# Splitting one rounding in the last, narrower supertile of two feed-forward networks, and moving one copy from ScalarE to VectorE

## The chip, the cores and the metric

The kernel runs on one core of one Trainium2 chip. The metric is the device time of one execution in microseconds (us), the median of several runs. In what follows TensorE is PE in the rows (its weight loads are PEld), VectorE is DVE, ScalarE is ACT, GpSimd is POOL and SyncE is SP.

## The reference

Attention without softmax, then two feed-forward networks over the 6016 tokens that come out of it:

```
scores = (1/3008) * z @ z.T ; attn = max(scores, 0)**2 ; x0 = u * (attn @ v)      # 2 batches x 3008 tokens, 256 wide
h = x0 @ w_in1 ; x1 = (h - tanh(h)) @ w_out1                                     # 256 -> 2048 -> 256
h = x1 @ w_in2 ; g = h if h >= 1, 0 if h <= -1, else (h + 1)**2 / 4 ; out = g @ w_out2
```

All is fp32. The kernel keeps that precision by splitting each operand of a product into a rounded part (hi) and the rest (lo), and by multiplying hi with hi, hi with lo and lo with hi.

## The kernel before, in words

The first 440 us are attention; the change leaves them alone. Then the networks (net 0 and net 1) run as a list of 95 units, numbered here 0 to 94. A unit is one network, one supertile `s` of 1024 tokens, and one eighth `f` of the 2048 hidden features. Net 0 is units 0 to 47, net 1 units 48 to 94. There are six supertiles in each; the last has 896 tokens. A supertile is handled as two halves of `w` tokens, so `w` is 512, and 448 in the last one. The units of width 448 are 40 to 47 and 88 to 94; they are called narrow here.

A unit's first product is done by a scheme with seven block products instead of eight (`mult`, three matmuls each), in an order written out by hand in `Unit.emit`: A11 and A12 into banks Y and X, S1 into V, S2 onto Y, later S3 onto Y, A22 onto Y and S4 onto V. Between them ScalarE copies the state of Y to SBUF three times (`snap`: m1 after A11, u2 after S2, u3 after S3), because Y is added to again, and VectorE adds bank and copy to get the hidden values: `A.h` (half A, rows j = 0 and 1) and `B.h` (half B). So S2 may not start before m1 is copied, S3 not before u2, A22 not before u3.

The activation, the rounding and the second product of a unit are staggered: half A's `first` (tanh on ScalarE in net 0, a clamp on VectorE in net 1), `value` (VectorE) and, in net 0, `round` (ScalarE, makes `gha`) are issued at the end of the unit itself; half A's `rest` (VectorE, makes `gla`) and all of half B (`first`, `value`, `round` to `ghb`, `rest` to `glb`) are issued inside the next unit, where `p` is the unit before. The second product of unit `p` is `one` (8 matmuls of gha), `two` (4 of gla, 6 of ghb) and `three` (2 of ghb, 4 of glb), and its matmuls stand between the blocks of the next unit: A11, A12, S1, S2, `one`, S3, `two`, A22, S4, `three`. That makes 45 matmuls a unit. The order on each engine is the order of the code: no scheduler changes it, and each engine works its own list from the top.

`fill()` is called twice a unit. It pops one step of preparing the next supertile's input (`x_steps`: subtractions and rests on VectorE, roundings on ScalarE), or, where there is none, some steps of converting the next weights (`work`), or one transposition of results (`turn`, net 1). In net 0 every narrow unit has such steps; in net 1 there is one, the last step of `x_steps`, in the second call of unit 88, and there are four transpositions, in units 89 and 90. In the kernel before, the first `fill()` stands between `p.B.round` and `p.B.rest`, ahead of S3.

`empty` copies a finished supertile's four banks of sums (00, 10, 01, 11: feature half d, token half n) out of PSUM, two on ScalarE and two on VectorE, in the second unit of the next supertile; those banks are reused by the matmuls of `one` in that unit. At the networks' border this is unit 49.

Of the kernel before, what the change touches and what calls it, by code (L numbers as in the profile page):

```python
# [8 lines left out]
F32R = mybir.dt.float32r  # L9
# [6 lines left out]
P = 128  # L16
# [6 lines left out]
QT = 512  # L23
# [8 lines left out]
def attention_then_two_ffn(  # L32
# [40 lines left out]
    sp_p = ctx.enter_context(tc.tile_pool(name="split", bufs=3))  # L73
# [31 lines left out]
    def flush():  # L105
        for fn in deferred:
            fn()
        deferred.clear()
# [236 lines left out]
    for c in list(range(QC)) * B:  # L345
        n = 1 if c == QC - 1 else 2
# [11 lines left out]
    between = []  # L358
# [364 lines left out]
    def fill():  # L723

        if fills:
            step = fills.pop(0)
            for fn in step:
                if fn is not None:
                    fn()
            if len(step) == 1:  # L730
                work(CONVERT[1] / 2)
        else:
            work(CONVERT[1])
        due()

    def copy(out_, in_):
        nc.scalar.activation(out=out_, in_=in_, func=AF.Copy)  # L737

    def add(out_, x, bank):
        nc.vector.tensor_tensor(out=out_, in0=x, in1=bank, op=ALU.add)  # L740

    class Half:
# [26 lines left out]
                out=t, in0=self.h[self.at(j)], in1=t, op=ALU.subtract if self.net == 0 else ALU.max,  # L769
            )  # L770

        def round(self, js=(None,)):
            self.hi = sp_p.tile([P, 2, 512], F32R, tag="hi", name=f"gh{self.nm}")
            for j in js:
                copy(self.hi[self.at(j)], self.t[self.at(j)])

# [15 lines left out]
    class Unit:  # L792
# [59 lines left out]
        def emit(self, p, att=None):  # L852

            w = self.w
            before = p and p.net == 1 and p.f == 0 and p.s and p.before
            self.before = p
            self.late = self.net == 1 or att is not None
            one, two, three = p.parts_list if p else ([], [], [])
            Y = self.bank()
            self.mult(Y, A11, "b11", True)  # L860
            m1 = self.snap("m1", Y)
            if p and p.late:
                p.A.round()
            if p and p.before and p.before.net == 0:
                p.before.empty(0)
            X = self.bank()
            self.mult(X, A12, "b21", True)
            if p:
                if p.net == 1:
                    p.B.first()  # L870
                p.A.rest()
                p.B.first() if p.net == 0 else p.B.square(1 if before else None)
            if att:
                for fn in att[2][:5]:
                    fn()
            self.A = Half(self.net, w, "a")
            if not (p and p.late):
                add(self.A.h[:, 0, :w], m1, X[:, :w])
            V = self.bank()
            self.mult(V, S1, "t1", True)  # L880
            if att:
                for fn in att[2][5:]:
                    fn()
                got = []
                inside.append(lambda: self.mult(Y, S2, "t2"))
                inside.append(lambda: got.append(self.snap("u2", Y)))
                att[0]()
                u2 = got[0]
            else:
                self.mult(Y, S2, "t2")  # L890
                u2 = self.snap("u2", Y)
            if before:
                before.empty(1, lambda: p.B.square(0))
            if p:
                for j in (1, 0) if before else (None,):
                    p.B.value(j)
                if p.late:
                    add(self.A.h[:, 0, :w], m1, X[:, :w])
            for fn in one[:4] if before else one:
                fn()  # L900
            if p:
                p.B.round((1, 0) if before else (None,))
                if self.i > 1:
                    fill()
                else:
                    scales.pop()()
                    due()
                    due()
                p.B.rest()
            self.mult(Y, S3, "t3")  # L910
            if before:
                for fn in one[4:6] + two[:2] + one[6:]:
                    fn()
                two = two[2:]
            u3 = self.snap("u3", Y)
            add(self.A.h[:, 1, :w], u3, V[:, :w])
            if self.net == 1 or att:
                self.A.first()
            for fn in two:
                fn()  # L920
            if att:
                self.A.value()
                att[1]()
            if self.i > 1:
                fill()
            if self.net == 1:
                self.A.square()
            self.mult(Y, A22, "t4")
            self.mult(V, S4, "b22")
            self.B = Half(self.net, w, "b")  # L930
            if self.net == 0 and not att:
                self.A.first()
            copy(self.B.h[:, 1, :w], Y[:, :w])
            if not att:
                self.A.value()
            if att:
                flush()
            add(self.B.h[:, 0, :w], u2, V[:, :w])
            for fn in three:
                fn()  # L940
            if not self.late:
                self.A.round()
            if p and p.net == 1:
                p.empty(0)
            self.parts_list = self.parts()

        def empty(self, n, between=None):

            if self.f < NPF - 1:
                return  # L950
            w = self.w
            if self.net == 0:
                for n in range(2):
                    for d in range(2):
                        bank = accs.pop((0, self.s, d, n))[:, :w]
                        y = raw_p.tile([P, 512], F32, tag="raw", name=f"y{d}{n}")
                        if d:
                            nc.vector.tensor_copy(out=y[:, :w], in_=bank)
                        else:
                            copy(y[:, :w], bank)  # L960
                        nc.sync.dma_start(out=kept[1, self.s][:, d, n * w : (n + 1) * w], in_=y[:, :w])
                return
            o = wide_p.tile([P, 2, 16, 32], F32, tag="wide", name="ot")
            for d in range(2):
                bank = accs.pop((1, self.s, d, n))
                y = raw_p.tile([P, 512], F32, tag="raw", name=f"y{d}{n}")
                copy(y, bank)
                if between and d == 0:
                    between()
                fills.append((lambda d=d, y=y: self.turn(o, d, n, y),))  # L970
# [153 lines left out]
    with tc.manual_schedule():  # L1124
# [64 lines left out]
        def work(amount):  # L1189

            if not (converts or posts):
                return
            state["credit"] = min(state["credit"] + amount, 2.0)
            if posts:
                cost, fn = posts.pop(0)
                fn()
                state["credit"] -= cost
            while converts and state["credit"] > 0 and len(posts) < 3:
                if state["step"] == 0:
                    next(converts[0])  # L1200
                elif state["step"] == 1 and len(converts) > 1:
                    next(converts[1])
                state["step"] += 1
                cost = next(converts[0], None)
                if cost is None:
                    converts.pop(0)
                    state["step"] = 1
                else:
                    state["credit"] -= cost
# [45 lines left out]
        def due():  # L1255

            now = [fn for k, fn in later if k <= 0]
            later[:] = [(k - 1, fn) for k, fn in later if k > 0]
            for fn in now:
                fn()  # L1260
# [73 lines left out]
        p = None  # L1334
        for i, (net, s, f) in enumerate(units):
            if f == 0:
                more = (net, s + 1) if (net, s + 1, 0) in units else (1, 0) if net == 0 else None
# [9 lines left out]
            p = u  # L1347
# [70 lines left out]
```

## Time and profile before

| | us |
|---|---|
| median of 3 runs (1419.55 to 1420.5) | 1420.18 |
| the profiled execution | 1417.62 |
| its span, first to last instruction | 1415.8 |
| TensorE busy in the span | 1408.6 |
| VectorE busy | 1243.9 |
| ScalarE busy | 996.3 |
| mean granted TensorE clock (share of full speed) | 0.999 |

TensorE's matmuls are pipelined, so its busy share says little on how close it is to its limit. What it loses is better read from the spacing of its weight loads: in an undisturbed narrow unit 45 loads follow each other every 0.203 us, 9.12 us in all, in a 512-wide unit every 0.227 us, 10.20 us.

### The profile page before, as it was taken

The page shows a single profiled execution, that of the slowest core. Times are in us where ns is not written, and L with a number is a line of the kernel's source. Part 1 is how long each engine was busy: PE and PEld are TensorE (multiplying, and loading weights), DVE is VectorE, ACT ScalarE, POOL GpSimd, SP SyncE. Part 2 cuts the span into 40 slices and gives each one's busy share as a digit, 9 for nine tenths or more (in the row PEclk, how much of TensorE's full clock was granted, in tenths as well). Part 3 has the DMA queues.
Part 4 walks back from the last instruction along what each step waited for, and adds up shares of the span by engine and source line. Part 5 has one row for each costly group of instructions (what it writes and reads, how often), then busy time and mean ns, then how long its engine had stood idle before and what let it go on. Part 6 is the DMA issues. An engine that isn't in the chain of part 4 may idle for free.

```text
span 1415.8 us, 21846 instructions
## 1 busy us (share of the span) xinstructions
PE 1408.6 (99%) x8206; PEld 1173.7 (83%) x8206; DVE 1243.9 (88%) x1557; ACT 996.3 (70%) x1258; POOL 116.0 (8%) x169
## 2 busy tenths in 40 slices
PE   9999999999999999999999999999999999999998
PEld 7888888888888888888888889988888888888897
DVE  8888899788898989899889889989898898988887
ACT  8888758888765767667676767666666666666664
POOL 0111110022110010110201110000000000000000
PEclk9999999999999999999999999999999999999999
DMA  8788897599989557484847667572564653546461
GB/s 231 249 279 256 234 237 190 177 283 270 257 220 318 198 195 254 167 309 134 314 147 271 230 224 276 173 289 89 176 225 178 208 189 109 184 157 222 148 208 27
DMA packets 229546, 301.02 MB, mean 213 GB/s; under 512 B 111152, under 2 KB 166192, under 8 KB 229440
## 3 DMA queue, kind: packets, MB, share of 16 engines
q1 hardware_dynamic: 213088, 258.01, 57.6%
q0 software_dynamic: 11520, 40.96, 8.1%
q8 instruction: 64, 1.05, 0.3%
q10 hardware_dynamic: 4832, 0.66, 0.3%
q14 instruction: 42, 0.34, 0.1%
HBM read 225.77 MB, written 73.79 MB: 212 GB/s over the span
## 4 chain that ended last, share of the span: by engine, by line
PE 60%; issue 36%; DVE 1%; ACT 1%; DMA 1%; POOL 0%; SPq 0%; POOLq 0%; DVEq 0%; ACTq 0%
PE acc L825 17%; PE acc L537 16%; PE m L806 15%; PE acc L526 7%; PE sc L449 4%; DMA packed<-plin 0%; ACT r L475 0%; PE acc L532 0%; DVE lo L434 0%; PE warm L1122 0%; ACT hi L483 0%; DVE am L416 0%; POOL win L282 0%; POOL packed L295 0%; DVE lo L499 0%
## 5 line engine op out<-in xcount | busy, mean ns | idle before, releaser
L806 PE MATMUL m<-xht,w 128*128 128x512 f32 (+1 forms) x760 | 231.2, 385 | 0.0
L825 PE MATMUL acc<-ghb,w 128*128 128x512 f32 (+1 forms) x760 | 200.8, 386 | 0.0
L537 PE MATMUL acc<-hi,v 64*128 64x512 f32 (+1 forms) x1588 | 195.5, 382 | 0.2
L825 PE MATMUL acc<-gha,w 128*128 128x512 f32 (+1 forms) x760 | 187.1, 386 | 0.0
L537 PEld LDWEIGHTS acc<-hi,v 64*128 64x128 f32 x1588 | 148.5, 184 | 29.2 <-DVE y L592 1.3
L825 PEld LDWEIGHTS acc<-gha,w 128*128 128x128 f32 x760 | 142.4, 188 | 27.5 <-ACT y L737 0.4
L825 PEld LDWEIGHTS acc<-ghb,w 128*128 128x128 f32 x760 | 141.2, 188 | 29.0 <-ACT ghb L737 0.7
L806 PEld LDWEIGHTS m<-xht,w 128*128 128x128 f32 x760 | 142.7, 188 | 26.4
L806 PE MATMUL m<-xlt,w 128*128 128x512 f32 (+1 forms) x380 | 147.2, 387 | 0.0
L779 DVE TENSOR_TENSOR gla<-ta,gha 128x1024 fp32r<-128x1024 f32 (+1 forms) x95 | 114.4, 1204 | 36.7 <-ACT gha L737 36.0
L737 ACT ACTIVATE ghb<-tb 128x1024 fp32r<-128x1024 f32 (+3 forms) x100 | 99.8, 1004 | 63.0 <-DVE tb L768 63.0
L768 DVE TENSOR_TENSOR ta<-ha,ta 128x1024 f32<-128x1024 f32 (+1 forms) x95 | 114.2, 1202 | 32.6 <-ACT ta L764 27.5
L779 DVE TENSOR_TENSOR glb<-tb,ghb 128x1024 fp32r<-128x1024 f32 (+1 forms) x95 | 114.0, 1200 | 18.1 <-ACT ghb L737 17.9
L737 ACT ACTIVATE u<-m 128x512 f32<-128x512 f32 (+1 forms) x190 | 110.3, 580 | 26.3 <-PE m L806 25.4
L737 ACT ACTIVATE gha<-ta 128x1024 fp32r<-128x1024 f32 (+1 forms) x95 | 98.9, 1041 | 35.0 <-DVE ta L768 34.8
L768 DVE TENSOR_TENSOR tb<-hb,tb 128x1024 f32<-128x1024 f32 (+3 forms) x100 | 114.7, 1147 | 6.5 <-ACT tb L753 2.2
L806 PE MATMUL m<-xhb,w 128*128 128x512 f32 (+1 forms) x380 | 115.6, 386 | 0.0
L764 ACT ACTIVATE ta<-ta 128x1024 f32<-128x1024 f32 (+1 forms) x47 | 49.2, 1046 | 85.4 <-DVE ta L755 85.4
L537 PE MATMUL acc<-lo,v 64*128 64x512 f32 (+1 forms) x772 | 104.9, 382 | 0.2 <-DVE lo L434 0.2
L475 ACT ACTIVATE r<-sc 128x1024 f32<-128x1024 f32 (+1 forms) x83 | 84.4, 1016 | 28.4 <-PE sc L449 28.0
L825 PE MATMUL acc<-gla,w 128*128 128x512 f32 (+1 forms) x380 | 101.3, 386 | 0.0
L825 PE MATMUL acc<-glb,w 128*128 128x512 f32 (+1 forms) x380 | 101.1, 385 | 0.0
(139 smaller groups left out, 2566.1 us busy)
## 6 DMA issues: line engine op xcount, KB each, us to landing
w<-packed SPq DMA_DIRECT2D x288, 512.0 KB, 5.9
mir<-ax SPq DMA_DIRECT2D x50, 512.0 KB, 4.6
m<-mir SPq DMA_DIRECT2D x200, 128.0 KB, 4.6
xr<-kept SPq DMA_DIRECT2D x20, 512.0 KB, 6.9
packed<-phin POOLq DMA_DIRECT2D x16, 512.0 KB, 5.7
packed<-plin POOLq DMA_DIRECT2D x16, 512.0 KB, 6.1
widein<-in_moe_w_in_dram POOLq DMA_DIRECT2D x15, 512.0 KB, 6.9
wideout<-in_moe_w_out_dram POOLq DMA_DIRECT2D x15, 512.0 KB, 7.7
```

Source lines behind the costliest of these rows:

```text
L449: nc.tensor.matmul(ps[:, j, :n], zs[b, g][half, x, k0 : k0 + P], q[half, y, :n], start=(k == 0), stop=(k == 2))
L475: nc.scalar.activation(out=r[s], in_=ps[s], func=AF.Relu)
L526: nc.tensor.matmul(acc[d][h].rearrange("p (i q) -> p i q", i=2), lhsT, g[half, j], start=start, stop=stop)
L537: nc.tensor.matmul(acc[d][h][:, :n], lhsT, g[half, j, :n], start=start, stop=stop and (h == 1 or not closes))
L737: nc.scalar.activation(out=out_, in_=in_, func=AF.Copy)
L764: nc.scalar.activation(out=t, in_=t, func=AF.Square, scale=0.5, bias=0.5)
L768: nc.vector.tensor_tensor(out=t, in0=self.h[self.at(j)], in1=t, op=ALU.subtract if self.net == 0 else ALU.max,)
L779: nc.vector.tensor_tensor(out=self.lo[self.s], in0=self.t[self.s], in1=self.hi.bitcast(F32)[self.s], op=ALU.subtract)
L806: nc.tensor.matmul(bank[:, : self.w], self.win[wp][:, block, :], xop[self.net, self.s][x][xp], start=start and i == 0, stop=True, skip_gro ...
L825: nc.tensor.matmul(self.acc(d, n)[:, : self.w], self.wout[:, part, j, d * P : (d + 1) * P], g[:, at, : self.w], start=start, stop=stop,)
```

## The change

Three edits. In a narrow unit (other than the second unit of a supertile in net 1, which is unit 89) the rounding of half B goes in two pieces: row j = 1 where the whole rounding stood, row j = 0 after S3 is issued and u3 is copied. In these units `p.B.rest` and the first `fill()` are issued behind the addition that reads u3, no longer ahead of S3. Unit 89 keeps its order and loses its first `fill()`: its four transpositions move on by one call each. In unit 49 VectorE copies banks 00, 10 and 01 and ScalarE bank 11 (before: ScalarE 00 and 01, VectorE 10 and 11).

```diff
-        def round(self, js=(None,)):
-            self.hi = sp_p.tile([P, 2, 512], F32R, tag="hi", name=f"gh{self.nm}")
+        def round(self, js=(None,), more=False):
+            if not more:
+                self.hi = sp_p.tile([P, 2, 512], F32R, tag="hi", name=f"gh{self.nm}")
...
+            narrow = w < QT and not before
...
-                p.before.empty(0)
+                p.before.empty(0, by_vector=3 if p.late else 2)
...
-                p.B.round((1, 0) if before else (None,))
-                if self.i > 1:
-                    fill()
-                else:
+                p.B.round((1, 0) if before else (1,) if narrow else (None,))
+                if self.i <= 1:
                     scales.pop()()
                     due()
                     due()
-                p.B.rest()
+                elif w == QT:
+                    fill()
+                if not narrow:
+                    p.B.rest()
             self.mult(Y, S3, "t3")
...
             u3 = self.snap("u3", Y)
+            if narrow:
+                p.B.round((0,), more=True)
             add(self.A.h[:, 1, :w], u3, V[:, :w])
+            if narrow:
+                p.B.rest()
+                fill()
...
-                        if d:
+                        if d if by_vector == 2 else 2 * n + d < by_vector:
                             nc.vector.tensor_copy(out=y[:, :w], in_=bank)
```

TensorE's and GpSimd's lists stay as they are. VectorE's list in unit 43, a narrow unit of net 0, before (gla, tb and glb are unit 42's, ha and ta unit 43's; xlb, t241 and plout belong to the two fills):

```order
L779 TENSOR_TENSOR gla_10359<-ta_10330,gha_10341 128x2x448
L740 TENSOR_TENSOR ha_10363<-m1_10353,m_10355 128x448
L768 TENSOR_TENSOR tb_10361<-hb_10329,tb_10361 128x2x448
L695 TENSOR_TENSOR xlb1_0_10385<-xr1_0_0_10046,xhb1_0_10298 128x1024
L779 TENSOR_TENSOR glb_10389<-tb_10361,ghb_10383 128x2x448
L740 TENSOR_TENSOR ha_10363<-u3_10394,m_10365 128x448
L658 TENSOR_TENSOR t241_0_10407<-xr1_0_1_10047,t131_0_10296 128x512
L291 TENSOR_TENSOR plout1_6_10409<-wout1_6_10226,phout1_6_10319 128x512
L768 TENSOR_TENSOR ta_10420<-ha_10363,ta_10420 128x2x448
```

And the same place of the same engine with the change:

```order
L780 TENSOR_TENSOR gla_10362<-ta_10333,gha_10344 128x2x448
L740 TENSOR_TENSOR ha_10366<-m1_10356,m_10358 128x448
L768 TENSOR_TENSOR tb_10364<-hb_10332,tb_10364 128x2x448
L740 TENSOR_TENSOR ha_10366<-u3_10391,m_10368 128x448
L780 TENSOR_TENSOR glb_10395<-tb_10364,ghb_10386 128x2x448
L695 TENSOR_TENSOR xlb1_0_10397<-xr1_0_0_10046,xhb1_0_10309 128x1024
L658 TENSOR_TENSOR t241_0_10411<-xr1_0_1_10047,t131_0_10307 128x512
L291 TENSOR_TENSOR plout1_6_10413<-wout1_6_10228,phout1_6_10322 128x512
L768 TENSOR_TENSOR ta_10424<-ha_10366,ta_10424 128x2x448
```

The addition that reads u3 moves ahead of the fill's xlb and of glb, which now stand between it and ta. ScalarE's list in the same unit, before (gha is unit 42's; m1, u2 and u3 are the copies of bank Y):

```order
L737 ACTIVATE gha_10341<-ta_10330 128x2x448
L737 ACTIVATE m1_10353<-m_10349 128x448
L753 ACTIVATE tb_10361<-hb_10329 128x2x448
L737 ACTIVATE u2_10372<-m_10349 128x448
L737 ACTIVATE ghb_10383<-tb_10361 128x2x448
L679 ACTIVATE xht131_0_10387<-t131_0_10296 128x1024
L737 ACTIVATE u3_10394<-m_10349 128x448
L753 ACTIVATE ta_10420<-ha_10363 128x2x448
```

And with the change:

```order
L737 ACTIVATE gha_10344<-ta_10333 128x2x448
L737 ACTIVATE m1_10356<-m_10352 128x448
L753 ACTIVATE tb_10364<-hb_10332 128x2x448
L737 ACTIVATE u2_10375<-m_10352 128x448
L737 ACTIVATE ghb_10386<-tb_10364 128x448
L737 ACTIVATE u3_10391<-m_10352 128x448
L737 ACTIVATE ghb_10386<-tb_10364 128x448
L679 ACTIVATE xht131_0_10399<-t131_0_10307 128x1024
L753 ACTIVATE ta_10424<-ha_10366 128x2x448
```

The copy u3 moves ahead of half the rounding and of the fill's xht. VectorE's list at the border, unit 49, as a piece of the difference (line numbers are the only change in the gla row):

```order
 L768 TENSOR_TENSOR ta_10843<-ha_10811,ta_10843 128x1024
 L740 TENSOR_TENSOR hb_10866<-u2_10820,m_10813 128x512
-L958 COPY y10_10893<-acc10_10193 128x448
-L958 COPY y11_10899<-acc11_10199 128x448
-L755 TENSOR_SCALAR tb_10906<-hb_10866 128x1024
-L779 TENSOR_TENSOR gla_10908<-ta_10843,gha_10888 128x1024
+L966 COPY y00_10898<-acc00_10191 128x448
+L966 COPY y10_10901<-acc10_10194 128x448
+L966 COPY y01_10904<-acc01_10197 128x448
+L755 TENSOR_SCALAR tb_10914<-hb_10874 128x1024
+L780 TENSOR_TENSOR gla_10916<-ta_10851,gha_10896 128x1024
```

Three copies instead of two stand ahead of half B's clamp and of gla.

## Rows read from the trace of the kernel before

**Rows 1.** The page's busy time: us, share of the span, instructions.

```profile
PE 1408.6 (99%) x8206; PEld 1173.7 (83%) x8206; DVE 1243.9 (88%) x1557; ACT 996.3 (70%) x1258; POOL 116.0 (8%) x169
```

**Rows 2.** Waits of PEld, 850 to 945 us: us in total, times, longest.

```profile
PEld acc L825 <- ACT y L737: 0.4, 1, 0.4
PEld acc L825 <- ACT ghb L737: 0.4, 1, 0.4
PEld m L806 <- ACT m L737: 0.2, 1, 0.2
PEld m L806 <- ACT u L737: 0.2, 1, 0.2
```

**Rows 3.** The same view, 1328 to 1395 us.

```profile
PEld m L806 <- DVE ha L740: 0.3, 1, 0.3
PEld acc L825 <- ACT ghb L737: 0.3, 1, 0.3
```

**Rows 4.** Timeline, PEld, unit 43 into 44: start, us, instruction, idle before.

```profile
879.12 0.19 PEld L806 LDWEIGHTS m<-xlt,w 128*128 128x128 f32 x1
...
884.18 0.19 PEld L806 LDWEIGHTS m<-xlb,w 128*128 128x128 f32 x1
...
886.01 0.19 PEld L806 LDWEIGHTS m<-xlt,w 128*128 128x128 f32 x1
```

**Rows 5.** Timeline, VectorE, unit 43.

```profile
877.92 1.08 DVE L768 TENSOR_TENSOR tb<-hb,tb 128x896 f32<-128x896 f32 x1
878.92 1.22 DVE L695 TENSOR_TENSOR xlb<-xr,xhb 128x1024 fp32r<-128x1024 f32 x1
880.05 1.08 DVE L779 TENSOR_TENSOR glb<-tb,ghb 128x896 fp32r<-128x896 f32 x1
881.40 0.62 DVE L740 TENSOR_TENSOR ha<-u,m 128x448 f32<-128x448 f32 x1 [0.26 <-ACT u L737]
881.94 0.69 DVE L658 TENSOR_TENSOR t<-xr,t 128x512 f32<-128x512 f32 x1
...
883.14 1.08 DVE L768 TENSOR_TENSOR ta<-ha,ta 128x896 f32<-128x896 f32 x1
```

**Rows 6.** Timeline, ScalarE, units 43 and 44.

```profile
875.39 0.95 ACT L737 ACTIVATE gha<-ta 128x896 fp32r<-128x896 f32 x1 [1.04 <-DVE ta L768]
876.25 0.52 ACT L737 ACTIVATE m<-m 128x448 f32<-128x448 f32 x1
...
887.02 0.55 ACT L737 ACTIVATE u<-m 128x448 f32<-128x448 f32 x1 [0.44 <-PE m L806]
```

**Rows 7.** VectorE by stretches from ta to ta, units 40 to 47: length, busy (instructions), clock, DMA.

```profile
874.27:883.14 8.87, 8.12 (x11) 1.00 0.59 237
...
891.66:900.90 9.24, 7.79 (x11) 1.00 0.18 57
900.90:910.89 9.99, 9.30 (x14) 1.00 0.47 160
...
sum 75.24, DVE 68.31; mean DVE 8.54
```

**Rows 8.** Timeline, PEld, unit 48, first matmuls of S2.

```profile
922.90 0.19 PEld L806 LDWEIGHTS m<-xlt,w 128*128 128x128 f32 x1 [0.23 <-ACT m L737]
923.01 0.42 PEld L806 LDWEIGHTS m<-xht,w 128*128 128x128 f32 x2
```

**Rows 9.** Timeline, VectorE, unit 49.

```profile
931.46 1.15 DVE L958 COPY y<-acc 128x448 f32<-128x448 f32 x2
932.53 0.68 DVE L755 TENSOR_SCALAR tb<-hb 128x1024 f32<-128x1024 f32 x1
```

**Rows 10.** Timeline, ScalarE, unit 49, and unit 89's rounding in two pieces.

```profile
933.04 0.97 ACT L737 ACTIVATE y<-acc 128x448 f32<-128x448 f32 x2
933.89 1.07 ACT L764 ACTIVATE tb<-tb 128x1024 f32<-128x1024 f32 x1
...
1344.60 1.05 ACT L737 ACTIVATE ghb<-tb 128x448 fp32r<-128x448 f32 x2
```

More of the change, by code (lines that the diff above doesn't have):

```diff
@@ L945, in emit, with empty @@
             self.parts_list = self.parts()
-        def empty(self, n, between=None):
+        def empty(self, n, between=None, by_vector=2):
             if self.f < NPF - 1:
```

## The prediction

> **What bounds the kernel now.** I read the page's busy times first. TensorE is busy 1408.6 of 1415.8 us [rows 1], but pipelined matmuls hide in that share, so I went on to what its weight loads wait for. Around the eight narrow units of net 0 and the border that view has four waits, 1.2 us together [rows 2]; around the narrow units of net 1 it has two, 0.6 us [rows 3]. The stretches that the change touches therefore run at TensorE's own pace, and all that can be won there is under 2 us. What can be lost has no such bound, so the question is how much slack stands behind each instruction that moves.
>
> The timeline of one unit gives it. In unit 43 the loads of S3 begin at 879.12; call this T. The next unit begins at 884.18, 25 matmuls later, which is 0.2024 us for each [rows 4]. S2 of that next unit begins at 886.01, T + 6.89, nine matmuls after the unit's start [rows 4]. S2 may not begin before ScalarE has copied bank Y (m1), and in net 0 ScalarE's list has half A's rounding (gha) just ahead of m1. Gha waits for VectorE's ta: it idled 1.04 us for it and m1 started 0.86 after gha started [rows 6]. So there is a loop from VectorE back to TensorE: S3, u3, the addition that reads u3, ta, gha, m1, the next S2. In unit 42 to 43 m1 ended at 876.25 + 0.52 = 876.77, about 0.1 before S2 was due. At unit 48 the loop already bites: S2 waits 0.23 us for m1 [rows 8]. That slack of about 0.1 us is what the change spends.
>
> **The change part by part.**
>
> *VectorE's order in the narrow units of net 0 (40 to 47).* Before, VectorE filled its time before u3 with the first fill step and glb: in unit 43 xlb from 878.92, glb from 880.05, and only then the addition at 881.40 [rows 5]. With the change the addition stands first, so VectorE idles from the end of tb until u3 is copied, and glb and the first fill step come after it, ahead of ta. They leave cover and enter the loop.
>
> The new time from T to the next S2, by rows: a Y copy starts 1.01 after its product's first load (u2: 887.02 against 886.01 [rows 4, 6]) and takes 0.55, since half a rounding ahead of it no longer holds it; 0.03 to the addition, whose pitch is 0.54 (881.40 to 881.94); glb with the pitch of a 896-wide operation, 1.00 (877.92 to 878.92); then the unit's whole fill work F; ta 1.08 [rows 5]; 0.04 to gha; 0.86 to m1, 0.52 for it [rows 6]; 0.05 to S2. The sum is 5.68 + F, and S2 is due at T + 6.89. A delayed load is followed by the next after 0.11 us instead of 0.20 (922.90 to 923.01 [rows 8]), so TensorE wins back about 0.1 of each wait. The loss of a unit is F - 1.3 us.
>
> F comes from VectorE's busy time from ta to ta, less its seven standing operations: ta 1.00, the additions 0.62, 0.54 and 0.54, gla and tb 1.00 each, glb 1.08, together 5.78 (pitches of [rows 5]; the one before an idle time counts in full). Unit 43 has 8.12 - 5.78 = 2.34; the least is unit 45 with 2.0, the most unit 46 with 3.5 [rows 7]. No unit stays under 1.3. Over all eight, busy time is 68.31; less 8 x 5.78, less 0.7 for unit 40's operations of 1024 and 1.2 for unit 41's two bank copies, F is 20.2 us in all. Less 8 x 1.3 that leaves 9.8.
>
> Two corrections. In unit 40 the second product is still 512 wide and in unit 48 the first, so S2 comes due later, by 0.39 and 0.22; with glb and m1 longer there too, this takes off 0.4. And what these units lose already (0.2 at unit 48 [rows 8], 0.1 in the rest) goes into the new wait. The first term is 9.8 - 0.4 - 0.3 = +9.1 us. If VectorE's operations run back to back more tightly than I count, F falls by up to 0.3 a unit and the term to 6.5; if gha or m1 are delayed further by the fill's rounding on ScalarE, which now stands behind the second piece, it rises, by at most 0.3 a unit, to 11.5. I take 9.0, between the two and nearest to the rows.
>
> *The rounding in two pieces.* Two pieces of 448 take 1.05 together [rows 10] where one of 896 takes 0.95 (the gha row of [rows 6]): 0.1 us more on ScalarE, which is busy 70% [rows 1]. The second piece starts behind u3, at about T + 1.45, and ends at T + 2.0. TensorE needs it after 3 + 4 + 4 matmuls, at T + 2.23. The margin is 0.2 us; I cost it at nothing, with a bound of 0.2 in each of 14 units, 2.8 us, if the piece comes late. Glb is needed after 21 matmuls, at T + 4.25, and ends by T + 3.2.
>
> *The narrow units of net 1.* Here half A's rounding stands behind m1, so the loop is open, and there is hardly a fill step to move. The addition comes 0.4 earlier, glb 0.5 later than before, and the clamp behind both where it was. The waits of [rows 3] go: unit 88's for ghb, since its first piece is ready 0.45 sooner, and unit 89's for the addition, whose transposition has left. I take -0.5 us, between 0 and -0.6.
>
> *The border, unit 49.* VectorE's copies have a pitch of 0.54 ((932.53 - 931.46) / 2 [rows 9]), ScalarE's of 0.43 ((933.89 - 933.04) / 2 [rows 10]). The Trainium skill, Advanced Engine Details and Errata, section The Read-Write Bubble, says that ScalarE is closer to PSUM and VectorE to SBUF and advises to use them so; by that rule this move is against the grain, and the trace agrees with its two pitches. By rule or by row the moved bank costs 0.54 on VectorE and gives 0.43 back on ScalarE. TensorE's wait of 0.4 for the first copied bank [rows 2] goes. But VectorE's clamp of half B starts 0.54 later, at 933.07, and ends at 933.76; ScalarE's square, which began at 933.89 [rows 10], can begin at 933.8. U2, tb and ghb hang on that square, and the waits for them [rows 2] stay but for 0.1. What is won at gha is given back at S3. I take -0.1, between +0.3 and -0.8 (all the waits of unit 49).
>
> The sum is 9.0 + 0 - 0.5 - 0.1 = +8.4 us. The profiled execution took 1417.62 us, 2.6 us under the median of the runs; against it the change gives 1426.0, against the median of 1420.18 it gives 1428.6 us, +0.6%.
>
> **The rivals.**
>
> A. No change: the loop has more slack than I read, because VectorE and ScalarE catch up in the idle time that they have. For it speaks that VectorE idles about a tenth of its time in these units (68.31 busy of 75.24 [rows 7]). Against it: that idle time stands ahead of u3, where nothing queued behind the addition can use it. The time would be 1420.2 us.
>
> B. Faster: the waits of [rows 2, 3] vanish and nothing takes their place. Their 1.8 us, less 0.1 for each of six, are 1.2 us: 1419.0 us. It decides if the net 0 units lose less than 1.2 / 8 = 0.15 each, that is if F is under 1.45 in the mean; the rows say 2.5. The Trainium skill, Perfetto Trace Analysis, section Optimizing Scalar/DVE Operations, says that where ScalarE or VectorE are not saturated but cause bubbles on other engines, breaking up instructions may let work finish sooner. Such bubbles are 0.2 to 0.4 us here, six of them; the rule names the gain of the split and not the price of the order that comes with it.
>
> C. Slower still: the second piece of ghb comes late too, with a price of 2.8 us on top (its margin of 0.2 gone in all 14 units): 1431.4 us. The new waits shift S3 and the rounding together, so I see no reason for it, but the margin is thin.
>
> **How the numbers follow.** My forecast has a chance of 0.80, A 0.08, B 0.05 and C 0.07. The range is that of the forecast: its first term 6.5 to 11.5 less 0.6, so +5.0 at the low end, and at the high end +11.3, which takes in C: 1425.0 to 1431.5 us. A measurement of this kernel can tell 0.2%, 2.8 us, from no change. All of the forecast's range and C lie above that, A and B below: slower 0.87; same 0.10 (A, and most of B, whose 1.2 us is within the bound); faster 0.03 (B with more than the waits that I can see).
>
> **What would show it.** In the changed kernel's profile TensorE's weight loads of S2 should wait for ScalarE's m1 in each of units 41 to 48, 0.5 to 2.2 us each and some 9 us in all, the most at unit 47 (behind the long fills of unit 46). VectorE should idle about 1.8 us ahead of the addition that reads u3 in each, released by ScalarE's u3. Units 41 to 47 should be about 10.2 us long in the mean instead of 9.12; those of net 1 should stay at 9.12. TensorE's wait for a bank copy at unit 49 should be gone and the waits for u2 and ghb should still stand there. The forecast is wrong if S2's loads wait for nothing: then m1 was early in spite of a late ta. It is wrong in size if the clock granted to TensorE, 1.00 in all of these stretches [rows 7], falls in the new waits.

## The result, and the profile after

| | before | after |
|---|---|---|
| median (runs) | 1420.09 us (6: 1419.25 to 1420.61) | 1429.02 us (6: 1428.15 to 1429.86) |
| profiled execution | 1417.62 us | 1429.64 us |
| its span | 1415.8 us | 1427.9 us |

The change makes the kernel slower: ratio 1.0064, 95% interval 1.0051 to 1.0076. The forecast was 1428.6 us in a range of 1425.0 to 1431.5.

The page's busy times hardly move against [rows 1]; VectorE and ScalarE do the same work in a longer span:

```profile
PE 1413.5 (99%) x8206; PEld 1174.8 (82%) x8206; DVE 1244.5 (87%) x1558; ACT 996.7 (70%) x1271; POOL 116.1 (8%) x169
```

The time shows in what the weight loads wait for. After the change, between 850 and 955 us (units 41 to 49; us in total, times, longest):

```profile
PEld m L807 <- ACT m L737: 10.4, 8, 2.5
PEld acc L826 <- ACT ghb L737: 0.4, 1, 0.4
PEld m L807 <- ACT u L737: 0.4, 1, 0.4
```

Where [rows 2] had one wait of 0.2 us for m1 there are eight with 10.4 us. The wait for a bank copy (y) is gone, those for ghb and u2 at the border are there. In net 1 (1335 to 1408 us), against [rows 3]:

```profile
PEld m L807 <- ACT u L737: 0.4, 2, 0.2
PEld acc L826 <- ACT gha L737: 0.2, 1, 0.2
```

The loop can be followed in unit 43, as in [rows 4 to 6]. TensorE after the change, loads of S3, of the next unit's first product, and of its S2:

```profile
882.32 0.19 PEld L807 LDWEIGHTS m<-xlt,w 128*128 128x128 f32 x1
...
887.38 0.19 PEld L807 LDWEIGHTS m<-xlb,w 128*128 128x128 f32 x1
...
890.33 0.19 PEld L807 LDWEIGHTS m<-xlt,w 128*128 128x128 f32 x1 [1.14 <-ACT m L737]
890.44 0.39 PEld L807 LDWEIGHTS m<-xht,w 128*128 128x128 f32 x2
```

VectorE in the same unit:

```profile
881.28 1.09 DVE L768 TENSOR_TENSOR tb<-hb,tb 128x896 f32<-128x896 f32 x1
883.90 0.62 DVE L740 TENSOR_TENSOR ha<-u,m 128x448 f32<-128x448 f32 x1 [1.53 <-ACT u L737]
884.44 1.08 DVE L780 TENSOR_TENSOR glb<-tb,ghb 128x896 fp32r<-128x896 f32 x1
885.44 1.22 DVE L695 TENSOR_TENSOR xlb<-xr,xhb 128x1024 fp32r<-128x1024 f32 x1
...
887.78 1.09 DVE L768 TENSOR_TENSOR ta<-ha,ta 128x896 f32<-128x896 f32 x1
```

And ScalarE:

```profile
883.32 0.55 ACT L737 ACTIVATE u<-m 128x448 f32<-128x448 f32 x1 [0.34 <-PE m L807]
883.76 0.57 ACT L737 ACTIVATE ghb<-tb 128x448 fp32r<-128x448 f32 x1
...
888.90 0.95 ACT L737 ACTIVATE gha<-ta 128x896 fp32r<-128x896 f32 x1 [2.34 <-DVE ta L768]
889.76 0.52 ACT L737 ACTIVATE m<-m 128x448 f32<-128x448 f32 x1
```

VectorE idles 1.53 us for u3 and only then does the addition, glb and the fill's three operations; ta starts at 887.78, T + 5.46 (it was T + 4.02). Gha, m1 and S2 follow as the sum had it: S2 at 890.33, T + 8.01, where 5.68 + F gives 5.68 + 2.34 = 8.02.

The lengths of the units, each the distance between the first loads of A11, in us. "Again" is a second profile of the kernel before, "third" a third one of the kernel after:

| unit | before | before again | after | after, third | net0_only | both_out |
|---|---|---|---|---|---|---|
| 41 | 9.14 | 9.21 | 10.35 | 10.39 | 10.35 | 9.14 |
| 42 | 9.12 | 9.30 | 10.42 | 10.38 | 10.55 | 9.12 |
| 43 | 9.12 | 9.30 | 9.81 | 9.81 | 9.73 | 9.12 |
| 44 | 9.12 | 9.30 | 10.15 | 10.15 | 10.15 | 9.12 |
| 45 | 9.12 | 9.30 | 10.15 | 10.15 | 10.15 | 9.12 |
| 46 | 9.12 | 9.30 | 9.55 | 9.55 | 9.68 | 9.12 |
| 47 | 9.12 | 9.30 | 13.11 | 11.55 | 11.47 | 9.19 |
| 48 | 9.82 | 9.72 | 11.19 | 11.20 | 11.19 | 9.69 |
| 49 | 10.88 | 10.87 | 10.78 | 10.77 | 10.84 | 10.89 |
| 88 | 9.93 | 9.93 | 9.77 | 9.77 | 9.95 | 9.95 |
| 89 | 9.45 | 9.47 | 9.34 | 9.34 | 9.45 | 9.45 |
| 90 to 93 | 36.57 | 37.20 | 37.15 | 37.15 | 36.92 | 36.92 |

Two things in it were not in the sum. Unit 47 took 13.11 us in the first profile after, 1.6 more than in the third with the same wait (the prediction named a falling clock only as a way to be wrong in size). And the kernel before has two paces: 9.12 or 9.30 us for the same undisturbed unit. Both are taken up below.

### The profile page after: what moved, and what is told of

Read it like the earlier page. It is cut to its first block, busy times and chain, and to the rows that moved or that the text cites. A ratio compares the mean times of both kernels' runs of the same rounds, so it can differ in the third digit from the quotient of the medians.

```text
span 1427.9 us, 21870 instructions
## 1 busy us (share of the span) xinstructions
PE 1413.5 (99%) x8206; PEld 1174.8 (82%) x8206; DVE 1244.5 (87%) x1558; ACT 996.7 (70%) x1271; POOL 116.1 (8%) x169
## 4 chain that ended last, share of the span: by engine, by line
PE 60%; issue 36%; DVE 2%; ACT 1%; SPq 0%; POOL 0%; DMA 0%; POOLq 0%; DVEq 0%
PE acc L537 18%; PE acc L826 16%; PE m L807 14%; PE acc L526 8%; PE sc L449 4%; DVE glb L780 1%; DVE ta L768 0%; SPq L397 0%; PE acc L532 0%; PE warm L1130 0%; ACT u L737 0%; DMA ub<-in_u_dram 0%; ACT gha L737 0%; ACT m L737 0%; PE acc L554 0%
## 5 line engine op out<-in xcount | busy, mean ns | idle before, releaser
L737 ACT ACTIVATE ghb<-tb 128x1024 fp32r<-128x1024 f32 (+2 forms) x114 | 102.5, 905 | 64.8 <-DVE tb L768 64.8
```

## The experiments

The theory: what stands on VectorE between u3 and ta in net 0 is paid in full, less 1.3 us a unit. The rivals: that the split or the early addition itself costs, that net 1 or the border carry the loss, or that chance (clock, pace) does. Edits are against the kernel after unless said otherwise. The first four ran beside 21 runs of the kernel before (1420.15 us), the next four beside 21 (1419.07), the last three beside 15 (1419.57).

**net0_only**: net 0's narrow units changed, all else as before.

```diff
-            narrow = w < QT and not before
+            narrow = w < QT and self.net == 0
...
-                p.before.empty(0, by_vector=3 if p.late else 2)
+                p.before.empty(0, by_vector=2)
...
-                elif w == QT:
+                elif not narrow:
```

> Only the narrow units of net 0 are changed (units 40 to 47); net 1 and the border stand as before. Theory (the loop S3, u3, addition, ta, gha, m1, S2 pays for all VectorE work behind the addition): TensorE's S2 loads wait for m1 in units 41 to 48, about 10 us of waits, and the time is 8.5 to 10.5 us over that of the kernel before, within 1 us of the changed kernel's. Rival (net 1 or the border carries a good part of the loss): at least 2 us less than the changed kernel.

1429.05 us, ratio 1.0063 (1.0049 to 1.0076): the whole loss. Eight waits for m1, 10.2 us. The rival falls.

**fill_back**: net0_only with the first fill step ahead of S3 again (edit against net0_only).

```diff
-                elif not narrow:
+                else:
                     fill()
...
             if narrow:
                 p.B.rest()
-                fill()
```

> As net0_only, but the first fill step goes back ahead of S3; the rounding stays split, the addition and then glb stay as in the changed kernel. Theory: the first step's VectorE work (0.6 to 1.4 us a unit) is under cover again; a unit loses what its second step has over 1.3 us: 0.1 in unit 42, 0.9 in 46, 0.1 in 47, the others nothing, in all about +1 us over the kernel before, and no clock drop. Rival (the split or the early addition is what costs): S2 still waits in every unit, +5 us or more.

1421.88 us, ratio 1.0014 (1.0005 to 1.0023): +1.7 us where +1 was expected, and 7 us less than net0_only. Moving one step back (in unit 43 one operation on VectorE, xlb, and one on ScalarE, xht) undoes four fifths of the loss, as the theory has it and the rival (+5) does not. ScalarE's part of the step is not what cost: in unit 43 after the change gha still idled 2.34 us for ta. The rest of the miss is in the loads' waits (848 to 960 us):

```profile
PEld m L807 <- ACT m L737: 2.5, 5, 1.0
PEld acc L826 <- ACT ghb L737: 1.5, 5, 0.4
```

The fill step has a rounding on ScalarE too, and the edit puts that back ahead of u3. U3 and the second piece of ghb come late in four units (42, 43, 45, 47), u3 at T + 1.42 to T + 1.51. In unit 42 of this kernel ScalarE did xhb between ghb's first piece and u3:

```profile
871.63 1.04 ACT L679 ACTIVATE xhb<-xr 128x1024 fp32r<-128x1024 f32 x1
872.58 0.52 ACT L737 ACTIVATE u<-m 128x448 f32<-128x448 f32 x1
873.00 0.57 ACT L737 ACTIVATE ghb<-tb 128x448 fp32r<-128x448 f32 x1
```

**no_split**: net0_only with half B rounded in one piece ahead of S3 (edit against net0_only).

```diff
-                p.B.round((1, 0) if before else (1,) if narrow else (None,))
+                p.B.round((1, 0) if before else (None,))
...
-            if narrow:
-                p.B.round((0,), more=True)
```

> As net0_only, but half B is rounded in one piece ahead of S3; only the VectorE order (addition, glb, first fill step) is changed. Theory: the order alone carries the loss; in the slowed loop the whole rounding starts about 0.1 us after S3's first load and is done as u3 can start, so the time is that of net0_only within 0.5 us. Rival (the split brings u3 forward and so gives part back): u3 comes 0.35 us later in eight units, 2.8 us slower than net0_only.

1429.48 us, ratio 1.0066 (1.0053 to 1.0078), 0.4 us over net0_only, within its spread. The order of VectorE's list is the cause, and the split of the rounding neither costs nor gives anything that can be measured here: u3 starts at T + 1.01 in units 42 to 46 without it too.

**both_out**: fill_back, and the second fill step goes to the unit's end (edit against fill_back).

```diff
-            if self.i > 1:
+            if self.i > 1 and not narrow:
                 fill()
...
             if not self.late:
                 self.A.round()
+            if narrow:
+                fill()
```

> As fill_back, and the second fill step is issued behind gha's rounding at the unit's end, so that only the addition and glb stand between u3 and ta. Theory: 5.7 us from S3's first load to the next S2, due at 6.9: no wait for m1 in units 41 to 48, and the time is that of the kernel before less up to 0.4 us (1419.7 to 1420.1). Rival (the fill steps only move the wait to another engine's list, to gla, tb or ghb): new waits of TensorE for gla or ghb, 2 us or more.

1418.99 us, ratio 0.9991 (0.9983 to 1.0000): as fast as the kernel before or a little faster. No wait for m1 is left; only the border's waits and one more for ghb remain (848 to 960 us):

```profile
PEld acc L826 <- ACT ghb L737: 0.6, 2, 0.4
PEld acc L826 <- ACT y L737: 0.4, 1, 0.4
PEld m L807 <- ACT u L737: 0.2, 1, 0.2
```

The fill's rounding stands ahead of u3 on ScalarE as in fill_back, but u3 is hardly late: T + 1.01 to T + 1.15 in units 41 to 46, T + 1.37 in unit 47. Half B comes sooner here: ghb's first piece starts at T - 0.28 in unit 43, and in unit 42 of fill_back at T + 0.04. ScalarE in unit 43 of this kernel, where S3's first load is at 878.82:

```profile
878.54 0.58 ACT L737 ACTIVATE ghb<-tb 128x448 fp32r<-128x448 f32 x1 [0.40 <-DVE tb L768]
879.02 1.04 ACT L679 ACTIVATE xht<-t 128x1024 fp32r<-128x1024 f32 x1
879.97 0.52 ACT L737 ACTIVATE u<-m 128x448 f32<-128x448 f32 x1
```

With fill_back this separates the two fill steps: each is harmless where it does not stand between u3 and ta.

**border_only**: only the copies at the border.

```diff
-            narrow = w < QT and not before
+            narrow = False
...
-                elif w == QT:
+                else:
                     fill()
```

> Only the copies at the border are changed (VectorE 00, 10, 01; ScalarE 11). Theory: TensorE's wait for the first copied bank goes and comes back at S3 as a wait for u2, since the square behind VectorE's later clamp starts no earlier; -0.1 us, no difference that can be measured. Rival (the wait for the bank was the cost): -0.4 to -0.8 us and no wait at S3 in unit 49.

1418.34 us, ratio 0.9998 (0.9989 to 1.0006): no difference that can be measured. Unit 49 was 10.49 us long, 0.38 shorter than in the second profile of the kernel before; of the wait for u2 0.16 was left and that for ghb stood as it was:

```profile
936.24 0.19 PEld L807 LDWEIGHTS m<-xlt,w 128*128 128x128 f32 x1 [0.16 <-ACT u L737]
...
938.11 1.22 PEld L826 LDWEIGHTS acc<-ghb,w 128*128 128x128 f32 x6 [0.42 <-ACT ghb L737]
```

That is more than the 0.1 expected and next to the rival's 0.4; against the rival stands only that the wait at S3 did not vanish. The full change, with unit 49 at 10.78, kept the 0.1.

**net1_only**: only the narrow units of net 1.

```diff
-            narrow = w < QT and not before
+            narrow = w < QT and not before and self.net == 1
...
-                p.before.empty(0, by_vector=3 if p.late else 2)
+                p.before.empty(0, by_vector=2)
...
-                elif w == QT:
+                elif w == QT or self.net == 0:
```

> Only the narrow units of net 1 are changed (88, 90 to 94, and unit 89 without its first fill step). The forecast said -0.5 us from the waits of units 88 and 89. The changed kernel's profile shows those two units shorter by 0.16 and 0.11 us but units 90 to 93 longer by 0.08 to 0.22. Theory now: the transpositions, moved one call on, stand behind glb and ahead of the clamp and delay gha in unit 92, and loads come every 0.207 us instead of 0.203 in three units; sum +0.1 to +0.4 us, not to be told from no change by the time alone. Rival: units 90 to 93 were longer because of what went before in net 0; then they are 9.12 us here and the sum is -0.4.

1418.34 us, ratio 0.9993 (0.9984 to 1.0002): not to be told from no change. Unit 88 took 9.79 us, unit 89 9.29, units 90 to 93 9.30, 9.20, 9.31 and 9.13. The 9.30 of unit 90 is found in the kernel before too (its second profile), so my theory's "0.207 instead of 0.203" was not the change's doing; the wait for gha in unit 92, 0.2 us, is. The rival's 9.12 did not come either: three of the four units are longer with net 0 left as before.

**long_wait**: net0_only with four additions behind glb in unit 43 that nothing reads (edit against net0_only).

```diff
                 p.B.rest()
+                if self.i == 43:
+                    for _ in range(4):
+                        d = raw_p.tile([P, 512], F32, tag="raw", name="spare")
+                        nc.vector.tensor_tensor(out=d[:, :w], in0=p.B.t[:, 0, :w], in1=p.B.t[:, 1, :w], op=ALU.add)
                 fill()
```

> As net0_only, with four additions of 448 that nothing needs put behind glb in unit 43 (about 2.1 us of VectorE work in the loop). Theory of the loop: unit 44's wait for m1 grows from 1.1 to about 3.3 us. On the clock: in the changed kernel ten matmuls after unit 47's wait of 2.54 us ran at 373 ns spacing, half the clock, and none after the waits of up to 1.6 us. If a long wait is the cause, the matmuls after unit 44's wait run at 373 ns too, and the time is 2.1 + 1.5 to 2 us over net0_only; if the drop belongs to unit 47's place or to chance, it is 2.1 us over and unit 44 runs at 203 ns.

Unit 44 took 12.21 us, 2.06 more than in net0_only: four pitches of 0.53 are 2.1, so VectorE work in the loop is paid one for one. Its loads:

```profile
892.82 0.19 PEld L807 LDWEIGHTS m<-xlt,w 128*128 128x128 f32 x1 [3.16 <-ACT m L737]
892.93 0.39 PEld L807 LDWEIGHTS m<-xht,w 128*128 128x128 f32 x2
893.34 1.61 PEld L826 LDWEIGHTS acc<-gha,w 128*128 128x128 f32 x8
```

Eight loads in 1.61 us after a wait of 3.16: full clock in this execution. The time, 1431.96 us, ratio 1.0089 (1.0074 to 1.0104), is 12.9 us over the kernel before that ran beside it; net0_only was 8.9 over its own. Of the 4.0 us between them the loop explains 2.1. The profiled run, 1430.32, was the lowest of four, and the other three lay 1.55 to 1.73 higher, about what a drop of the clock costs. No profile shows those three. So the times fit the first case of the expectation and the profile the second, and what a long wait does to the clock stays open.

**before_again**: the kernel before, unchanged.

> The kernel before, unchanged, for a second profile. The first profiled execution took 1417.62 us, 2.5 us less than the median of its timed runs; the profiles of before and after differ by 12.0 us and the medians by 8.9. If the first profile was a quick execution, this one takes about 1420 and shows where 2.5 us more lie (longer spacing of the loads or more waits); if profiles are quicker in general, it takes about 1417.6.

1419.68 us, so the first profile was a quick execution. There is no new wait in it; the loads of the narrow units come more slowly. Units 40 to 49 and 88 to 93 hold 1.7 of the 2.06 us between the two profiles. The first load of unit 43 and of unit 44:

```profile
875.39 0.19 PEld L806 LDWEIGHTS m<-xlb,w 128*128 128x128 f32 x1
...
884.69 0.19 PEld L806 LDWEIGHTS m<-xlb,w 128*128 128x128 f32 x1
```

9.30 us for 45 loads that nothing holds up, 0.207 each, where [rows 4] had 0.2024.

**all_three**: the change's border and net 1, with both_out's order in net 0.

```diff
+            inner = narrow and self.net == 0
...
-                elif w == QT:
+                elif w == QT or inner:
...
-                fill()
+                if not inner:
+                    fill()
...
-            if self.i > 1:
+            if self.i > 1 and not inner:
...
+            if inner:
+                fill()
```

> The changed kernel's border and net 1 together with both_out's order in net 0 (first fill step ahead of S3, second behind gha's rounding). Theory: both_out lost no time to m1 and took 1.2 us off the median, the border alone and net 1 alone had profiles 0.4 and 0.3 us shorter in units 49, 88 and 89; with all three no wait for m1 in units 41 to 48 and 1 to 2 us under the kernel before (ratio 0.9987 to 0.9993). Rival (the gains are only the pace that the loads happen to fall into): 0 to -0.5 us.

1418.72 us, ratio 0.9992 (0.9983 to 1.0001): 0.85 us under the kernel before where 1 to 2 were expected. No wait for m1; not better than both_out, and not clearly better than the kernel before. Unit 49 took 10.88 us here, so the border gave nothing. The gains of the border and of net 1 do not add up to something that can be measured.

**after_again and after_third**: the kernel after, unchanged, for the clock in unit 47.

> The changed kernel, unchanged, for a second profile. Six runs of it lay at 1428.2 to 1428.4 and at 1429.6 to 1429.9; the one profile, of a run of 1429.64, had unit 47's matmuls at half the clock for ten matmuls, 1.7 us. If the drop is what sets the two groups apart, a run near 1428.3 shows unit 47 at 11.4 us and one near 1429.8 at 13.1 us; if not, the two do not go together.

> The changed kernel once more, for a third profile, with the same two expectations: if the clock drop in unit 47 sets the two groups of times apart, its time and unit 47's length go together.

The three profiles of this kernel: 1429.64 and 1429.1 us with unit 47 at 13.11 and 13.18, and 1428.27 us with unit 47 at 11.55. Time and drop go together in all three, as the first expectation has it; three are few.

## Why the prediction was right, and where it was not

The mechanism and its place are as forecast: eight waits of S2 for m1 in units 41 to 48, 0.54 to 2.54 us each, VectorE idle for u3 ahead of the addition, the greatest wait in unit 47. Taking VectorE's first fill step out of the loop (fill_back) and then the second (both_out) took the loss away; adding work to the loop (long_wait) lengthened it by that work. Neither the split (no_split) nor net 1 nor the border (net0_only) has a part in it that can be measured.

*The first term, +9.1 us.* Against the first profile of the kernel before, units 41 to 48 lost 9.5 us in the third profile after (83.18 against 73.68 us, by the table) and 11.05 in the first. The term for a unit, F - 1.3, holds at unit 44 (1.04 forecast, 1.03 measured); it is too high at unit 46 (0.7 against 0.43) and a little low at unit 47 (2.2 against 2.35 to 2.43). At unit 46 it was F that was mis-sized: busy time counts in full the tail of an operation ahead of an idle time, unit 45 has three more of those than the sum took off, and by pitch its two fill operations are 0.60 + 1.14 = 1.74 us and not 2.0. The range has a slip: 6.5 less 0.6 is 5.9, not the 5.0 of its low end; the measured +8.9 lies inside either way.

*The second piece of ghb, cost nothing.* It ended at 884.33, T + 2.01 (forecast T + 2.0), and glb at 885.52, T + 3.2; no load of units 41 to 48 waited for them. Rival C did not come. It shows in fill_back, where u3 comes late: there the loads waited for ghb five times (1.5 us in all, the border's 0.4 among them).

*Net 1, -0.5 us: wrong.* The two named waits went and gave 0.16 and 0.11 us. The failed sentence is that the clamp stays where it was. In units 90 and 91 the transposition that moved one call on stands between glb and the clamp. VectorE in unit 91 after the change:

```profile
1376.27 1.09 DVE L780 TENSOR_TENSOR glb<-tb,ghb 128x896 fp32r<-128x896 f32 x1
1377.27 0.71 DVE L981 STREAM_TRANSPOSE ot<-y 128x512 f32<-128x512 f32 x1
1377.90 0.58 DVE L755 TENSOR_SCALAR ta<-ha 128x896 f32<-128x896 f32 x1
```

The clamp starts 0.6 later for it, the activation and gha with it, and in unit 92 TensorE waits for gha:

```profile
1381.70 1.51 PEld L826 LDWEIGHTS acc<-gha,w 128*128 128x128 f32 x8 [0.22 <-ACT gha L737]
```

I had called net 1's loop open because gha stands behind m1 there; it is open for m1, and gha itself has its own due time. The net of it is about 0.

*The border, -0.1 us.* Unit 49 took 10.78 us against 10.88. Three copies and the clamp on VectorE, after the change:

```profile
942.50 1.68 DVE L966 COPY y<-acc 128x448 f32<-128x448 f32 x3
944.10 0.69 DVE L755 TENSOR_SCALAR tb<-hb 128x1024 f32<-128x1024 f32 x1
```

ScalarE's square waits for that clamp:

```profile
944.07 0.53 ACT L737 ACTIVATE y<-acc 128x448 f32<-128x448 f32 x1
944.82 1.06 ACT L764 ACTIVATE tb<-tb 128x1024 f32<-128x1024 f32 x1 [0.21 <-DVE tb L755]
```

So the first bank's wait was gone and the wait at S3 grew to 0.40 us, as argued: given back one product later. In border_only 0.38 was won, because VectorE's copies started 0.74 us after the unit's first load there and 0.96 after it here. In all_three they started 1.11 after it, the wait at S3 was 0.53, and unit 49 took 10.88. I had not seen that the size depends on that.

*The level.* I added the forecast to the median of the runs as if a quick execution and a common one differed by a constant. They do not. The common one, as far as its one profile shows, is longer mostly because its undisturbed narrow units run at 9.30 us instead of 9.12, and units that wait for m1 go by the loop, whatever the pace. Against the second profile of the kernel before, units 41 to 48 lost only 8.45 us (83.18 - 74.73). The clock drop of unit 47, about 1.6 us in some executions, went the other way. The two cancel nearly. That 1428.6 came so close to 1429.02 us is luck: against the two profiles of the kernel before the first term alone is off by 0.4 and by 0.65 us.

*Rivals.* A and B put their hope in VectorE's idle time and in the waits that go. Idle time there was, 1.5 us a unit, but ahead of the addition, and only what is queued ahead of the addition can use it. The Trainium skill's rule that breaking up instructions may let work finish sooner (Perfetto Trace Analysis, Optimizing Scalar/DVE Operations) agrees with the trace of both_out: between u2 and u3 of unit 43 its ScalarE does what the kernel before does, but for the split, and u3 starts at T + 1.15 instead of T + 1.72, of which 0.19 is ghb's earlier start. After the change u3 came at T + 1.0, but so it did without the split (no_split, T + 1.01): in the delayed units it was the fill's rounding, gone from ahead of u3, that let it (with the split and that rounding ahead, in fill_back, u3 starts at T + 1.48). What was tied to the addition's place in VectorE's list cost many times what an earlier u3 could give.

## What to carry to other kernels

Before moving an operation to where its input is ready sooner, list what is queued behind it on that engine and which of that is on a loop back to the busiest engine: idle time ahead of a wait can only be filled by what stands ahead of that wait. Work that nobody needs soon (preparing the next tile) belongs in that gap, or behind the last operation of the loop. And take the time from more than one profile of the kernel before: a single quick execution shifts every difference.

## What the runs showed of the hardware that I had not expected

Undisturbed 448-wide matmuls keep one of two paces, 9.12 or 9.30 us for 45 of them (0.203 and 0.207 us each); the granted clock was 1.00 in unit 43 of the kernel before and in unit 90 after, one at each pace. Units 42 to 47 of the kernel before took 9.12 us each in one profile and 9.30 each in the other. The pace stays from unit to unit, and the changes that I followed came at a short delay, in either direction: in the first profile after the change unit 90 ran at 9.30, and in unit 91 a load came 0.02 us late and 0.203 followed; in the second profile of the kernel before a load of unit 41 came 0.06 late and 0.207 followed. What sets it is open.

In two of three profiles of the kernel after, TensorE ran at half its clock for about ten matmuls behind unit 47's wait. Its loads, after a wait of 2.54 us:

```profile
921.58 0.19 PEld L807 LDWEIGHTS m<-xlt,w 128*128 128x128 f32 x1 [2.54 <-ACT m L737]
921.69 0.39 PEld L807 LDWEIGHTS m<-xht,w 128*128 128x128 f32 x2
922.10 2.55 PEld L826 LDWEIGHTS acc<-gha,w 128*128 128x128 f32 x8
```

For about 1 us behind the wait the loads still follow each other at 0.20 us; then eight come at a spacing of 0.373, which is 448 columns at 1.2 GHz, the lower of the clock's two levels. The granted clock of that unit was 0.87 in the mean (length; busy time of PE, PEld, VectorE, ScalarE and GpSimd; clock; DMA):

```profile
917.23:930.34 13.11, 10.95 (x47) 9.68 (x45) 9.49 (x13) 6.58 (x10) 2.41 (x5) 0.87 0.99 357
```

The third profile had the same wait of 2.54 us and no drop:

```profile
921.57 0.19 PEld L807 LDWEIGHTS m<-xlt,w 128*128 128x128 f32 x1 [2.54 <-ACT m L737]
921.68 0.39 PEld L807 LDWEIGHTS m<-xht,w 128*128 128x128 f32 x2
922.09 1.61 PEld L826 LDWEIGHTS acc<-gha,w 128*128 128x128 f32 x8
```

Nor had the profiles of net0_only (2.42), no_split (2.54) and long_wait (3.16 and 2.54) a drop. So such a wait may bring it or not; what else it takes was not settled.

VectorE slows beside GpSimd. In unit 46 after the change its 512-wide scalar operations took 0.42 us until GpSimd began to add weights, and up to 0.69 then:

```profile
916.62 0.42 DVE L250 TENSOR_SCALAR eout<-wideout 128x512 uint32<-128x512 uint32 x1
916.95 0.69 DVE L252 TENSOR_SCALAR mout<-wideout 128x512 uint32<-128x512 uint32 x1
...
918.77 1.34 DVE L768 TENSOR_TENSOR ta<-ha,ta 128x896 f32<-128x896 f32 x1
```

```profile
916.85 2.32 POOL L282 TENSOR_TENSOR win<-win 128x128 f32<-128x128 f32 x4 [28.15 <-DVE win L270]
```

Ta, which runs into the end of these additions, took 1.34 us instead of 1.09. In unit 40 of the kernel before, with GpSimd idle, the same four scalar operations took 0.42 to 0.43 us each. The Trainium skill (Perfetto Trace Analysis, Optimizing Scalar/DVE Operations) says that the two engines share a read port of SBUF; the trace agrees, though it does not show the port itself. The slowing is part of why unit 46's fill work was the longest and unit 47's wait the greatest.
